# A fused linear-attention and channel-mix kernel: zero matmuls at the start, full transposes after a regrouping copy, later weight loads, and a re-tuned task order

## The chip, the cores and the metric

The kernel runs on one core of a Trainium2 chip. The metric is the device time of one execution in microseconds (us). Executions of one kernel differ, so each run is sorted into a state, "fast" or "slow" (over 1.5% above the fastest run of the same kernel). Comparisons use fast runs. Profiles give a "span", some 2 us shorter than the device time.

Engine names in the profile: PE is the matrix engine TensorE, PEld its weight loads (they overlap PE: 96.9 and 74.7 us busy in a span of 119.0 in the kernel before), DVE is VectorE, ACT is ScalarE, POOL is GpSimd, SP is the engine that only issues transfers here. "L187" is line 187 of the kernel that the profile belongs to; the same statement has other line numbers in other variants.

## The reference, cut to what matters

```python
def phi(x):                                   # q, k: (4 batches, 4 heads, 1088 tokens, 32)
    a = einsum('rd,bhsd->bhsr', S1, x)        # r = 8
    b = einsum('rd,bhsd->bhsr', S2, x)
    return outer(a, b).reshape(..., 64)
q_p, k_p = phi(q), phi(k)
kv  = einsum('bhsf,bhsd->bhfd', k_p, v);  z = k_p.sum(over tokens)
x   = (q_p @ kv) / (q_p . z + 1e-6)           # heads side by side: (4, 1088, 128)
x_prev = x shifted by one token
xk  = mu_k * x + (1 - mu_k) * x_prev;  xr likewise with mu_r
out = sigmoid(xr @ w_r) * (relu(xk @ w_k)**2 @ w_v)          # 128 -> 1024 -> 128
```

The whole k side of a batch must be summed before any x of that batch exists, and a token needs the x of its neighbour. The kernel works on two halves (two batches each), 17 tiles of 128 tokens per half, in groups of four tiles.

## The kernel before

Three parts matter. First, the loads and the transposes. k of the first half and q of the second come "head-wise" and are transposed on VectorE; k of the second half (`k1`) and q of the first (`q0`) come "token-wise" and are transposed on TensorE, one head (32 columns) at a time:

```python
    nc.gpsimd.tensor_copy(warm[:], hd["k00"][:R, 0, 0, :1])   # wait for the first tile
    load_tok("q0", q, nc.gpsimd, 1)
    load_tok("v1", v, nc.gpsimd, 1)
    nc.gpsimd.dma_start(mu_k[:], moe_mu_k.rearrange("d -> d ()"))
    nc.gpsimd.dma_start(wk[:], moe_w_k)                       # f32 to bf16 on the way
    ...
    def transp_tok(x, t0, t1):
        tp = bank["tp", x, t0] = psum.tile([P, 512], F32, name="tp", tag="aux")
        for t in range(t1 - t0):
            for h in range(H):
                nc.tensor.matmul(tp[D * h:D * h + D, t * P:t * P + P], tok[x][:, h, t0 + t, :], ident[:],
                                 skip_group_check=True, tile_position=(0, D * h))
```

Second, the names of the groups: `abp` is the projection of k, `kp` its outer product (VectorE), `kv` the accumulation, `zE` the sum z; `abwp`, `qp`, `qtp`, `xps`, `XK` are the steps from q to the mixed x; `h` is the first matmul of the channel mix, `o` the second, `rps` the gate, `osb` the output product.

Third, the order of all this is not written by hand. Each piece of work is a task with a length, needs and a priority `key`, and a small list scheduler at build time puts the tasks in a fixed order on each engine. The engines then run in that order:

```python
    PERIOD = 6.5
    for g in range(NQ):                       # a group of four query tiles
        due = (g - 1) * PERIOD - (50 if g < 2 else 0)
        task(("q1", g), "PE", 0.66 * f, ..., due - 9, opens=("aux", ("q", g)))
        task(("den", g), "DVE", 1.13, ..., due - 8)
        ...
        task(("xk", g), "DVE", 0.7, ..., due - 1, holds=[("x", g)])
    for g in range(NQ):
        x = [("xk", i) for i in range(min(g + 2, NQ))]        # the next group's x too
        for cp in range(4):
            key = g * PERIOD + cp * PERIOD / 4
            task(("mm1", g, cp), "PE", 0.43 * f, ..., x + ["dma_w"], key, opens=("h", ("h", g, cp)))
```

## Time and profile before

| | before |
|---|---|
| median of the device time | 122.8 us (121.62 to 123.44, 3 runs) |
| span of the profiled run (fast) | 119.0 us |
| TensorE busy, share of the span | 96.9 us, 81% |
| VectorE, ScalarE busy | 77.7 us, 67.3 us |
| loads done, by the 40 slices | about 28 us |

From the page of the kernel before: busy time per engine, then the span in 40 slices of 2.98 us (a digit is the busy share in tenths; PEclk the granted clock of TensorE; DMA the load of the transfer engines).

```profile
PE 96.9 (81%) x1594; PEld 74.7 (63%) x1594; DVE 77.7 (65%) x157; ACT 67.3 (57%) x117; POOL 8.9 (7%) x31
...
PE   0439998453999999799979999959969799789970
...
ACT  0402111000335477355599999777959869698950
...
PEclk9999999998699999999999999999999999999997
DMA  2999999991000000000000101002002002020212
```

TensorE is mostly full from the eleventh slice on, but not before, while the loads run. PEclk shows 9 also before the clock's first record (at 18.4 us in this trace), although the projections of that time take 423 ns a record against 278 ns for the same shape later. Before the first record the row says nothing, and the mean granted clock of a run counts that time as full speed (1.00 for 0 to 15 us in the table by windows). The next lines are from the chain of waits of the same profile (start, length, what):

```profile
20.43 0.49 PE kv L210 x21
20.93 1.59 issue
22.52 0.91 PE kv L210 x43
23.43 0.35 PE tp L169 x8
23.79 1.09 PE kv L210 x64
24.88 0.56 PE tp L169 x13
25.44 3.40 issue
28.84 1.49 PE tp L169 x19
```

Both gaps lie in the middle of a group of like matmuls, after 21 of 64 and after 13 of 32, so it is not data that is missing. Between them stand 43 + 8 + 64 + 13 = 128 matmul records, each with a weight-load record: 256. The groups of instructions, by shape (operation, output and inputs, count, then busy us and mean ns), give the price of the transposes:

```profile
L306 PE MATMUL qtp<-ident,qp 128*128 128x128 f32 x68 | 10.2, 277 | 0.0
...
L169 PE MATMUL tp<-ident,tok_q_69 128*32 128x128 f32 x136 | 6.3, 318 | 3.4 <-issue 3.4
L169 PE MATMUL tp<-ident,tok_k_68 128*32 128x128 f32 x136 | 4.5, 275 | 0.4 <-DMA tok_k_68<-in_k_dram 0.4
```

A full transpose (`qtp`) leaves one matmul record. The transpose by single heads needs four matmuls of two records each for the same tile: 272 records for 34 tiles. Why these leave two records each is not shown; they are the price seen here.

### The profile page before, as it was taken

The page shows a single profiled execution, that of the slowest core. Times are in us where ns is not written, and L with a number is a line of the kernel's source. Part 1 is how long each engine was busy: PE and PEld are TensorE (multiplying, and loading weights), DVE is VectorE, ACT ScalarE, POOL GpSimd, SP SyncE. Part 2 cuts the span into 40 slices and gives each one's busy share as a digit, 9 for nine tenths or more (in the row PEclk, how much of TensorE's full clock was granted, in tenths as well). Part 3 has the DMA queues.
Part 4 walks back from the last instruction along what each step waited for, and adds up shares of the span by engine and source line. Part 5 has one row for each costly group of instructions (what it writes and reads, how often), then busy time and mean ns, then how long its engine had stood idle before and what let it go on. Part 6 is the DMA issues. An engine that isn't in the chain of part 4 may idle for free.

```text
span 119.0 us, 3645 instructions
## 1 busy us (share of the span) xinstructions
PE 96.9 (81%) x1594; PEld 74.7 (63%) x1594; DVE 77.7 (65%) x157; ACT 67.3 (57%) x117; POOL 8.9 (7%) x31
## 2 busy tenths in 40 slices
PE   0439998453999999799979999959969799789970
PEld 0439997342788978478646777846646567556640
DVE  5465841000198993369778799859999686866870
ACT  0402111000335477355599999777959869698950
POOL 5196000050000000000000000000000000000000
PEclk9999999998699999999999999999999999999997
DMA  2999999991000000000000101002002002020212
GB/s 75 364 288 344 275 286 258 236 313 18 6 6 0 6 0 6 8 0 6 3 0 0 71 23 70 24 0 88 0 0 94 0 0 88 0 94 0 88 62 70
DMA packets 5262, 9.72 MB, mean 82 GB/s; under 512 B 1520, under 2 KB 1904, under 8 KB 5248
## 3 DMA queue, kind: packets, MB, share of 16 engines
q1 hardware_dynamic: 2976, 6.13, 16.3%
q0 software_dynamic: 1568, 1.71, 7.2%
q10 hardware_dynamic: 704, 1.67, 4.4%
q8 instruction: 12, 0.20, 0.7%
q14 instruction: 2, 0.02, 0.0%
HBM read 7.80 MB, written 2.23 MB: 84 GB/s over the span
## 4 chain that ended last, share of the span: by engine, by line
PE 56%; DMA 14%; DVE 13%; issue 7%; ACT 7%; ACTq 1%
DMA tok_k_68<-in_k_dram 14%; PE o L402 9%; PE tp L169 9%; PE h L381 8%; PE kv L210 7%; PE xps L344 6%; PE abwp L277 6%; PE qtp L306 5%; PE abp L181 4%; DVE osb L423 3%; DVE qp L189 2%; DVE XK L368 2%; DVE qpT L158 1%; PE rps L412 1%; PE rps L410 1%
## 5 line engine op out<-in xcount | busy, mean ns | idle before, releaser
L381 PE MATMUL h<-XK,wk 128*128 128x512 bf16 (+1 forms) x72 | 20.1, 367 | 3.9 <-DVE XK L368 3.2
L189 DVE TENSOR_TENSOR kp<-ab 128x1024 f32<-128x1024 f32 (+1 forms) x10 | 10.6, 1059 | 4.8 <-ACT ab L156 4.8
L156 ACT COPY ab<-abp 128x256 f32<-128x256 f32 (+1 forms) x10 | 3.4, 340 | 15.7 <-PE abp L181 15.7
L181 PE MATMUL abp<-SW,kT_136 128*128 128x64 f32 x34 | 7.8, 425 | 3.4 <-DVE kT_136 L163 3.4
L189 DVE TENSOR_TENSOR qp<-abw,an 128x1024 f32<-128x1024 f32 (+1 forms) x9 | 10.4, 1159 | 0.0
L306 PE MATMUL qtp<-ident,qp 128*128 128x128 f32 x68 | 10.2, 277 | 0.0
L344 PE MATMUL xps<-qpT,kvbd 128*64 128x256 f32 (+3 forms) x80 | 9.8, 359 | 0.1
L181 PEld LDWEIGHTS abp<-SW,kT_136 128*128 128x128 f32 x34 | 7.4, 331 | 3.7 <-DVE kT_136 L163 3.6
L381 PEld LDWEIGHTS <-wk 128*128 128x128 bf16 x72 | 5.9, 97 | 5.6 <-issue 4.7
L169 PE MATMUL tp<-ident,tok_q_69 128*32 128x128 f32 x136 | 6.3, 318 | 3.4 <-issue 3.4
L306 PEld LDWEIGHTS qtp<-ident,qp 128*128 128x128 f32 x68 | 7.8, 142 | 1.9 <-issue 0.4
L220 DVE TENSOR_TENSOR zE_140<-kv,mE 128x64 f32<-128x64 f32 x1 | 0.2, 225 | 12.9 <-PE kv L210 12.9
L210 PE MATMUL kv<-tok_v_66,kp 64*64 64x64 f32 x272 | 6.9, 261 | 1.6 <-issue 1.6
L156 ACT COPY qT_138<-tp 128x512 f32<-128x512 f32 (+1 forms) x4 | 2.0, 506 | 10.2 <-PE tp L169 10.2
L210 PEld LDWEIGHTS kv<-tok_v_66,kp 64*64 64x64 f32 x272 | 6.0, 170 | 2.7 <-issue 2.5
L423 DVE TENSOR_TENSOR osb<-o,r 128x512 f32<-128x512 f32 (+1 forms) x9 | 5.9, 658 | 1.9 <-PE o L402 1.8
L344 PEld LDWEIGHTS xps<-qpT,kvbd 128*64 128x64 f32 x80 | 4.7, 136 | 3.7 <-issue 1.0
L169 PEld LDWEIGHTS tp<-ident,tok_q_69 128*32 128x32 f32 x136 | 4.3, 127 | 4.3 <-issue 3.7
L156 ACT COPY qpT<-qtp 128x512 f32<-128x512 f32 x11 | 6.4, 597 | 0.7 <-PE qtp L306 0.7
L158 DVE COPY qpT<-qtp 128x512 f32<-128x512 f32 (+1 forms) x7 | 4.3, 614 | 2.6 <-PE qtp L306 2.6
L156 ACT COPY abw<-abwp 128x384 f32<-128x384 f32 (+1 forms) x9 | 4.2, 471 | 2.2 <-PE abwp L277 2.1
L181 PE MATMUL abp<-SW,kT_137 128*128 128x64 f32 x34 | 4.7, 278 | 0.8 <-DVE kT_137 L158 0.8
(240 smaller groups left out, 215.1 us busy)
## 6 DMA issues: line engine op xcount, KB each, us to landing
out_dram<-osb SPq DMA_DIRECT2D x7, 256.0 KB, 2.0
hd_k_70<-in_k_dram SPq DMA_DIRECT2D x1, 544.0 KB, 3.7
hd_k_71<-in_k_dram ACTq DMA_DIRECT2D x1, 544.0 KB, 5.6
tok_v_66<-in_v_dram SPq DMA_DIRECT2D x1, 544.0 KB, 8.5
tok_v_66<-in_v_dram ACTq DMA_DIRECT2D x1, 544.0 KB, 9.6
tok_k_68<-in_k_dram SPq DMA_DIRECT2D x1, 544.0 KB, 14.5
tok_k_68<-in_k_dram ACTq DMA_DIRECT2D x1, 544.0 KB, 16.8
tok_q_69<-in_q_dram SPq DMA_DIRECT2D x1, 544.0 KB
```

Source lines behind the costliest of these rows:

```text
L156: nc.scalar.copy(o, i)
L158: nc.vector.tensor_copy(o, i)
L169: nc.tensor.matmul(tp[D * h:D * h + D, t * P:t * P + P], tok[x][:, h, t0 + t, :], ident[:], skip_group_check=True, tile_position=(0, D * h))
L181: nc.tensor.matmul(p[:, t * 64:t * 64 + 64], kT[half][:, t0 + t, :], SW[:, 0, :, :2, :], skip_group_check=True)
L189: nc.vector.tensor_mul(o, _ap(a_, list(a_.ap[1:]) + [[0, R]]), _ap(b_, list(b_.ap[1:3]) + [[0, R]] + [b_.ap[3]]))
L210: nc.tensor.matmul(kv[hp:hp + 64, b2, (h // 2) * 64:(h // 2) * 64 + 64], f[rows, t - t0, h].rearrange("p i j -> p (i j)"), _ap(rhs, [[(H - ...
L277: nc.tensor.matmul(p[64 * b2:64 * b2 + 64, t * 96:t * 96 + 96], qT[half][:, T, 64 * b2:64 * b2 + 64], SW[:, 2 * half + b2].rearrange("p h ...
L306: nc.tensor.transpose(p[:, t * P:t * P + P], qp[g][:, t, 2 * pair:2 * pair + 2].rearrange("p h i j -> p (h i j)"), ident[:])
L344: nc.tensor.matmul(o[64 * pair:64 * pair + 64], kvbd[:, 2 * half + b2, pair, :], qpT[g, pair][:].rearrange("p t (b s) -> p t b s", b=2)[:, ...
L381: nc.tensor.matmul(h[:, c, :n * P], wk[:, (2 * cp + c) * P:(2 * cp + c + 1) * P], XK[:, 4 * g:4 * g + n, :].rearrange("p t s -> p (t s)"))
L402: nc.tensor.matmul(bank["o", g][:, t * P:t * P + P], k2[:, c, t * P:t * P + P], wv[:, 2 * cp + c, :], start=(cp == 0 and c == 0 and t == 0 ...
L423: nc.vector.tensor_mul(o[:, :n].rearrange("p t f -> p (t f)"), bank.pop(("o", g))[:, :n * P], rs[g][:, :n * P])
```

## The change

Its intent, in three named parts and one unnamed one: (1) 19 zero matmuls keep TensorE busy while the first tiles load; they are meant to have its clock up when work comes; (2) a ScalarE copy regroups the token-wise tiles so that a tile is transposed in one piece; (3) the weights are loaded after `v1`, in short runs, and the head tiles are padded so that their runs are short too; (4) the 20 constants of the task order are replaced by tuned ones, and the scheduler now models the buffer rings in SBUF, some of which are one buffer smaller, and starts from slightly different assumed durations and arrival times.

```diff
+    zps = psum.tile([P, 2, 512], F32, name="zps", tag="h")
+    def spin(count):
+        for _ in range(count):
+            nc.tensor.matmul(zps[:, 0, :], zero[:, :P], zero[:], skip_group_check=True)
+    spin(7)
 ...
-    wk = const.tile([P, DFF], BF16)
+    wk = const.tile([P, 4, 2 * P + 32], BF16)
 ...
     load_tok("v1", v, nc.gpsimd, 1)
+    nc.gpsimd.tensor_copy(warm[:], tok["v1"][:R, 0, 0, :1])       # waits for v1
     nc.gpsimd.dma_start(mu_k[:], moe_mu_k.rearrange("d -> d ()"))
-    nc.gpsimd.dma_start(wk[:], moe_w_k)
+    nc.gpsimd.dma_start(wk[:, :, :2 * P], moe_w_k.rearrange("p (c f) -> p c f", c=4))
 ...
+    spin(12)                                                     # after the matmuls on S1, S2
 ...
+        nc.scalar.copy(tall[x, t0][:, :n].rearrange("p t h d -> p h t d"), tok[x][:, :H, t0:t1, :])
 ...
-            for h in range(H):
-                nc.tensor.matmul(tp[D * h:D * h + D, t * P:t * P + P], tok[x][:, h, t0 + t, :], ident[:],
-                                 skip_group_check=True, tile_position=(0, D * h))
+            nc.tensor.transpose(tp[:, t * P:t * P + P], tall[x, t0][:, t].rearrange("p h d -> p (h d)"), ident[:])
 ...
+    K = dict(k1=-14.04, k1s=2.47, t=-25.79, q0=-80.88, q0s=14.85, early=55.2, q1=-10.84, den=-22.35, qp=-21.71, qt=-6.7,
+             num=-4.63, xp=7.46, xk=-15.83, gate=5.96, fin=-38.43, mm1=-1.19, mm2=-20.64, sq=-8.85, tq=86.38, P=3.65)
 ...   (every key is now written with these; rings of SBUF buffers are modelled like those of PSUM)
-    slots = {"aux": [0.0] * 2, "o": [0.0] * 2, "h": [0.0] * 2}
+    rings = dict(aux=2, o=2, h=2, tall=3, ab=3, kp=3, abw=3, an=3, qp=2, qpT0=2, qpT1=2, k1=3, k2=3, r=3)
```

More of the change, by code (lines that the diff above doesn't have):

```diff
@@ L67 @@
     tok = {x: const.tile([P, H + (x[0] == "v"), NT, D], F32, name="tok_" + x) for x in ("v0", "v1", "k1", "q0")}
-    hd = {x: const.tile([P, 2, NT, D], F32, name="hd_" + x) for x in ("k00", "k01", "q10", "q11")}
+    hd = {x: const.tile([P, 2, NT + 1, D], F32, name="hd_" + x) for x in ("k00", "k01", "q10", "q11")}
     def load_tok(x, src, eng, b2):
@@ L74, in load_hd @@
     def load_hd(x, src, eng):
-        eng.dma_start(hd[x][:], src[2 * int(x[1]) + int(x[2])].rearrange("h (a c t) d -> (h a) c t d", a=32, c=2))
+        eng.dma_start(hd[x][:, :, :NT], src[2 * int(x[1]) + int(x[2])].rearrange("h (a c t) d -> (h a) c t d", a=32, c=2))
+    zero = const.tile([P, 512], BF16)
+    nc.gpsimd.memset(zero[:], 0.0)
+    zps = psum.tile([P, 2, 512], F32, name="zps", tag="h")
[3 more added lines that the diff above has]
+    spin(7)
     S8 = const.tile([R, 2, D], F32)
@@ L163, in transp_hd, with regroup @@
             nc.vector.transpose(dst[:, t0:t1, 64 * b2 + c:64 * b2 + 64:2], hd[x][:, c, t0:t1, :])
+    tall = {}
+    def regroup(x, t0, t1):
+        n = t1 - t0
+        tall[x, t0] = work.tile([P, 4, H, D], F32, name="tall", tag="tall", bufs=3)
+        nc.scalar.copy(tall[x, t0][:, :n].rearrange("p t h d -> p h t d"), tok[x][:, :H, t0:t1, :])
     def transp_tok(x, t0, t1):
@@ L193, in k_feat @@
         ab = kab.pop((half, gi))
-        kp[half, gi] = work.tile([P, 4, H, R, R], F32, name="kp", tag="kp", bufs=4)
+        kp[half, gi] = work.tile([P, 4, H, R, R], F32, name="kp", tag="kp", bufs=3)
         outer(kp[half, gi][:, :n], ab[:, :n, :, 0, :], ab[:, :n, :, 1, :])
@@ L380, in mm1 @@
         for c in range(2):
-            nc.tensor.matmul(h[:, c, :n * P], wk[:, (2 * cp + c) * P:(2 * cp + c + 1) * P],
+            nc.tensor.matmul(h[:, c, :n * P], wk[:, cp, c * P:c * P + P],
                              XK[:, 4 * g:4 * g + n, :].rearrange("p t s -> p (t s)"))
@@ L385, in relu @@
         n = qn[g]
-        k1s[g, cp] = work.tile([P, 2, 512], BF16, name="k1", tag="k1", bufs=4)
+        k1s[g, cp] = work.tile([P, 2, 512], BF16, name="k1", tag="k1", bufs=3)
         nc.scalar.activation(k1s[g, cp][:, :, :n * P], bank.pop(("h", g, cp))[:, :, :n * P], RELU)
@@ L391, in square @@
         k1 = k1s.pop((g, cp))
-        k2s[g, cp] = work.tile([P, 2, 512], BF16, name="k2", tag="k2", bufs=4)
+        k2s[g, cp] = work.tile([P, 2, 512], BF16, name="k2", tag="k2", bufs=3)
         nc.vector.tensor_mul(k2s[g, cp][:, :, :n * P], k1[:, :, :n * P], k1[:, :, :n * P])
@@ L421, in fin @@
         n = qn[g]
-        o = work.tile([P, 4, P], F32, name="osb", tag="osb", bufs=3)
+        o = work.tile([P, 4, P], F32, name="osb", tag="osb", bufs=2)
         nc.vector.tensor_mul(o[:, :n].rearrange("p t f -> p (t f)"), bank.pop(("o", g))[:, :n * P], rs[g][:, :n * P])
@@ L435, with task @@
     tasks = {}
-    def task(name, eng, length, fn, need=(), key=0.0, opens=None, holds=()):
+    def task(name, eng, length, fn, need=(), key=0.0, opens=(), holds=()):
         tasks[name] = dict(eng=eng if isinstance(eng, tuple) else (eng,), len=length, fn=fn, need=list(need),
-                           key=key, opens=opens, holds=list(holds))
-    EV = {"ACT": 0.49, "DVE": 0.60}
-    arrive = {"S": 4.6, "k00": 5.5, "k01": 5.5, "v0": 8.5, "k1": 11.5, "q0": 14.5, "v1": 17.5, "q10": 19.0, "q11": 21.0,
-              "w": 24.0}
+                           key=key, opens=list(opens), holds=list(holds))
+    K = dict(k1=-14.04, k1s=2.47, t=-25.79, q0=-80.88, q0s=14.85, early=55.2, q1=-10.84, den=-22.35, qp=-21.71, qt=-6.7,
+             num=-4.63, xp=7.46, xk=-15.83, gate=5.96, fin=-38.43, mm1=-1.19, mm2=-20.64, sq=-8.85, tq=86.38, P=3.65)
+    EV = {"ACT": 0.50, "DVE": 0.62}
+    arrive = {"S": 4.6, "k00": 5.5, "k01": 5.5, "v0": 8.5, "k1": 11.5, "q0": 14.5, "v1": 17.5, "q10": 20.0, "q11": 22.0,
+              "w": 27.0}
     for x, t in arrive.items():
@@ L452 @@
             f = (t1 - t0) / 4
-            base = -100 + 4 * gi if half == 0 else -14 + 4 * gi
+            base = -100 + 4 * gi if half == 0 else K["k1"] + K["k1s"] * gi
             if half == 0:
@@ L456 @@
             else:
-                task(("ttk", gi), "PE", 0.86 * f, lambda e, t0=t0, t1=t1: transp_tok("k1", t0, t1), ["dma_k1"], base - 3,
-                     opens=("aux", ("tp", "k1", t0)))
+                task(("rk", gi), "ACT", 0.55 * f, lambda e, t0=t0, t1=t1: regroup("k1", t0, t1), ["dma_k1"], base + K["t"] - 1,
+                     opens=[("tall", ("tall", "k1", t0))])
+                task(("ttk", gi), "PE", 0.44 * f, lambda e, t0=t0, t1=t1: transp_tok("k1", t0, t1), [("rk", gi)], base + K["t"],
+                     opens=[("aux", ("tp", "k1", t0))])
@@ L459 @@
                 task(("ttke", gi), ("ACT", "DVE"), EV, lambda e, t0=t0, t1=t1: transp_out(e, kT[1], "k1", t0, t1),
-                     [("ttk", gi)], base - 3, holds=[("tp", "k1", t0)])
+                     [("ttk", gi)], base + K["t"], holds=[("tp", "k1", t0)])
+                tasks["ttk", gi]["holds"] += [("tall", "k1", t0)]
                 src = [("ttke", gi)]
             task(("kpj", half, gi), "PE", 0.89 * f, lambda e, h=half, g=gi: k_proj(h, g), src + ["dma_S"], base,
-                 opens=("o", ("ab", half, gi)))
+                 opens=[("o", ("ab", half, gi))])
@@ L464 @@
             task(("kab", half, gi), ("ACT", "DVE"), {"ACT": .27, "DVE": .33}, lambda e, h=half, g=gi: k_ab(e, h, g),
-                 [("kpj", half, gi)], base, holds=[("ab", half, gi)])
-            task(("kp", half, gi), "DVE", 1.15 * f + .05, lambda e, h=half, g=gi: k_feat(h, g), [("kab", half, gi)], base)
+                 [("kpj", half, gi)], base, holds=[("ab", half, gi)],
+                 opens=[("ab", ("abs", half, gi))])
+            task(("kp", half, gi), "DVE", 1.15 * f + .05, lambda e, h=half, g=gi: k_feat(h, g), [("kab", half, gi)], base,
+                 holds=[("abs", half, gi)], opens=[("kp", ("kps", half, gi))])
@@ L467 @@
             task(("kacc", half, gi), "PE", 1.15 * f, lambda e, h=half, g=gi: k_acc(h, g),
                  [("kp", half, gi), f"dma_v{half}"] + ([("kacc", half, gi - 1)] if gi else []), base,
-                 opens=("h", ("kv", half)) if gi == 0 else None, holds=[("kv", half)])
-        base = -80 if half == 0 else 4
+                 opens=[("h", ("kv", half))] if gi == 0 else (), holds=[("kv", half), ("kps", half, gi)])
+        base = -80 if half == 0 else K["k1"] + 4.5 * K["k1s"]
         task(("kz", half), "DVE", 0.22, lambda e, h=half: k_z(h), [("kacc", half, len(GR) - 1)], base, holds=[("kv", half)])
-        task(("kw", half), "PE", 0.3, lambda e, h=half: k_w(h), [("kz", half)], base, opens=("aux", ("w", half)))
+        task(("kw", half), "PE", 0.3, lambda e, h=half: k_w(h), [("kz", half)], base, opens=[("aux", ("w", half))])
@@ L477 @@
         f = (t1 - t0) / 4
-        task(("ttq", t0), "PE", 0.86 * f, lambda e, t0=t0, t1=t1: transp_tok("q0", t0, t1), ["dma_q0"], -78 + 6 * i,
-             opens=("aux", ("tp", "q0", t0)))
+        task(("rq", t0), "ACT", 0.55 * f, lambda e, t0=t0, t1=t1: regroup("q0", t0, t1), ["dma_q0"], K["q0"] - 1 + K["q0s"] * i,
+             opens=[("tall", ("tall", "q0", t0))])
+        task(("ttq", t0), "PE", 0.44 * f, lambda e, t0=t0, t1=t1: transp_tok("q0", t0, t1), [("rq", t0)], K["q0"] + K["q0s"] * i,
+             opens=[("aux", ("tp", "q0", t0))], holds=[("tall", "q0", t0)])
         task(("ttqe", t0), ("ACT", "DVE"), EV, lambda e, t0=t0, t1=t1: transp_out(e, qT[0], "q0", t0, t1), [("ttq", t0)],
-             -78 + 6 * i, holds=[("tp", "q0", t0)])
+             K["q0"] + K["q0s"] * i, holds=[("tp", "q0", t0)])
     for pc, (t0, t1) in enumerate(((9, NT), (0, 9))):
@@ L484 @@
             task(("tq", pc, b2), "DVE", 0.72, lambda e, b2=b2, t0=t0, t1=t1: transp_hd(qT[1], f"q1{b2}", t0, t1),
-                 [f"dma_q1{b2}"], -2 + 2 * pc + b2)
-    PERIOD = 6.5
+                 [f"dma_q1{b2}"], K["tq"] + 2 * pc + b2)
+    PERIOD = K["P"]
     for g in range(NQ):
         f = qn[g] / 4
-        due = (g - 1) * PERIOD - (50 if g < 2 else 0)
+        due = (g - 1) * PERIOD - (K["early"] if g < 2 else 0)
         need = []
@@ L496 @@
         halves = sorted({q_tile(4 * g + t)[0] for t in range(qn[g])})
-        task(("q1", g), "PE", 0.66 * f, lambda e, g=g: q_proj(g), dict.fromkeys(need), due - 9, opens=("aux", ("q", g)))
-        task(("q1e", g), ("ACT", "DVE"), {"ACT": .38, "DVE": .48}, lambda e, g=g: q_ab(e, g), [("q1", g)], due - 9,
-             holds=[("q", g)])
-        task(("den", g), "DVE", 1.13, lambda e, g=g: q_den(g), [("q1e", g)], due - 8)
-        task(("qp", g), "DVE", 1.15 * f + .05, lambda e, g=g: q_feat(g), [("den", g)], due - 7)
+        task(("q1", g), "PE", 0.83 * f, lambda e, g=g: q_proj(g), dict.fromkeys(need), due + K["q1"], opens=[("aux", ("q", g))])
@@ new lines @@
+        task(("q1e", g), ("ACT", "DVE"), {"ACT": .38, "DVE": .48}, lambda e, g=g: q_ab(e, g), [("q1", g)], due + K["q1"],
+             holds=[("q", g)], opens=[("abw", ("abw", g))])
+        task(("den", g), "DVE", 1.13, lambda e, g=g: q_den(g), [("q1e", g)], due + K["den"], holds=[("abw", g)],
+             opens=[("an", ("an", g))])
+        task(("qp", g), "DVE", 1.15 * f + .05, lambda e, g=g: q_feat(g), [("den", g)], due + K["qp"],
+             holds=[("abw", g), ("an", g)], opens=[("qp", ("qp", g))])
@@ L502 @@
         for pair in range(2):
-            task(("qt", g, pair), "PE", 0.44 * f, lambda e, g=g, r=pair: q_tr(g, r), [("qp", g)], due - 5,
-                 opens=("aux", ("t", g, pair)))
+            task(("qt", g, pair), "PE", 0.44 * f, lambda e, g=g, r=pair: q_tr(g, r), [("qp", g)], due + K["qt"],
+                 opens=[("aux", ("t", g, pair))], holds=[("qp", g)])
             task(("qte", g, pair), ("ACT", "DVE"), EV, lambda e, g=g, r=pair: q_trout(e, g, r), [("qt", g, pair)],
-                 due - 5, holds=[("t", g, pair)])
+                 due + K["qt"], holds=[("t", g, pair)], opens=[(f"qpT{pair}", ("qpT", g, pair))])
@@ L507 @@
         task(("num", g), "PE", 0.88 * f, lambda e, g=g: q_num(g), [("qte", g, 0), ("qte", g, 1)] + [("kkv", h) for h in halves],
-             due - 3, opens=("aux", ("x", g)))
-        task(("xp", g), "ACT", 1.1, lambda e, g=g: x_prev(g), [("num", g), "dma_w"], due - 2, holds=[("x", g)])
-        task(("xk", g), "DVE", 0.7, lambda e, g=g: x_mix(g), [("xp", g)] + ([("xp", g - 1)] if g else []), due - 1,
+             due + K["num"], opens=[("aux", ("x", g))], holds=[("qpT", g, 0), ("qpT", g, 1)])
@@ L511 @@
+        task(("xp", g), "ACT", 1.1, lambda e, g=g: x_prev(g), [("num", g), "dma_w"], due + K["xp"], holds=[("x", g)])
+        task(("xk", g), "DVE", 0.7, lambda e, g=g: x_mix(g), [("xp", g)] + ([("xp", g - 1)] if g else []), due + K["xk"],
              holds=[("x", g)])
@@ L516 @@
             key = g * PERIOD + cp * PERIOD / 4
-            task(("mm1", g, cp), "PE", 0.43 * f, lambda e, g=g, c=cp: mm1(g, c), x + ["dma_w"], key, opens=("h", ("h", g, cp)))
-            task(("relu", g, cp), "ACT", 0.92 * f, lambda e, g=g, c=cp: relu(g, c), [("mm1", g, cp)], key, holds=[("h", g, cp)])
-            task(("sq", g, cp), "DVE", 0.6 * f, lambda e, g=g, c=cp: square(g, c), [("relu", g, cp)], key)
-            task(("mm2", g, cp), "PE", 0.45 * f, lambda e, g=g, c=cp: mm2(g, c),
-                 [("sq", g, cp)] + ([("mm2", g, cp - 1)] if cp else []), key,
-                 opens=("o", ("o", g)) if cp == 0 else None, holds=[("o", g)])
@@ L523 @@
-        task(("gate", g), "PE", 0.45 * f, lambda e, g=g: gate(g), x + ["dma_w"], g * PERIOD + 3, opens=("aux", ("r", g)))
-        task(("sig", g), "ACT", 0.5 * f, lambda e, g=g: sigm(g), [("gate", g)], g * PERIOD + 3, holds=[("r", g)])
-        task(("fin", g), "DVE", 0.6 * f, lambda e, g=g: fin(g), [("mm2", g, 3), ("sig", g)], g * PERIOD + 7, holds=[("o", g)])
+            task(("mm1", g, cp), "PE", 0.43 * f, lambda e, g=g, c=cp: mm1(g, c), x + ["dma_w"], key + K["mm1"], opens=[("h", ("h", g, cp))])
@@ new lines @@
+            task(("relu", g, cp), "ACT", 0.92 * f, lambda e, g=g, c=cp: relu(g, c), [("mm1", g, cp)], key + K["mm1"], holds=[("h", g, cp)],
+                 opens=[("k1", ("k1", g, cp))])
+            task(("sq", g, cp), "DVE", 0.6 * f, lambda e, g=g, c=cp: square(g, c), [("relu", g, cp)], key + K["sq"],
+                 holds=[("k1", g, cp)], opens=[("k2", ("k2", g, cp))])
+            task(("mm2", g, cp), "PE", 0.45 * f, lambda e, g=g, c=cp: mm2(g, c),
+                 [("sq", g, cp)] + ([("mm2", g, cp - 1)] if cp else []), key + K["mm2"],
+                 opens=[("o", ("o", g))] if cp == 0 else (), holds=[("o", g), ("k2", g, cp)])
@@ L527 @@
+        task(("gate", g), "PE", 0.45 * f, lambda e, g=g: gate(g), x + ["dma_w"], g * PERIOD + K["gate"], opens=[("aux", ("r", g))])
+        task(("sig", g), "ACT", 0.5 * f, lambda e, g=g: sigm(g), [("gate", g)], g * PERIOD + K["gate"], holds=[("r", g)],
+             opens=[("r", ("rs", g))])
+        task(("fin", g), "DVE", 0.6 * f, lambda e, g=g: fin(g), [("mm2", g, 3), ("sig", g)], g * PERIOD + K["fin"], holds=[("o", g), ("rs", g)])
     HOP = 0.2
-    slots = {"aux": [0.0] * 2, "o": [0.0] * 2, "h": [0.0] * 2}
@@ L529 @@
-    turn = {r: 0 for r in slots}
+    rings = dict(aux=2, o=2, h=2, tall=3, ab=3, kp=3, abw=3, an=3, qp=2, qpT0=2, qpT1=2, k1=3, k2=3, r=3)
+    held = {r: [None] * n for r, n in rings.items()}
+    turn = dict.fromkeys(rings, 0)
     users = {}
     for n, t in tasks.items():
-        if t["opens"]:
-            users.setdefault(t["opens"][1], set()).add(n)
-        for b_ in t["holds"]:
-            users.setdefault(b_, set()).add(n)
+        for b_ in [b_ for _, b_ in t["opens"]] + t["holds"]:
+            users.setdefault(b_, []).append(n)
@@ L536 @@
     done, free, order = {}, {e: 0.0 for e in ("PE", "ACT", "DVE", "DMA")}, []
-    held = {r: [None] * len(s) for r, s in slots.items()}
     where = {}
@@ L551, in ready @@
             at = max(at, done[d] + (HOP if where[d] != e else 0.05))
-        if t["opens"]:
-            r = t["opens"][0]
+        for r, _ in t["opens"]:
             old = held[r][turn[r] % len(held[r])]
@@ L574 @@
         ln = t["len"][e] if isinstance(t["len"], dict) else t["len"]
-        if t["opens"]:
-            r, b_ = t["opens"]
+        for r, b_ in t["opens"]:
             held[r][turn[r] % len(held[r])] = b_
```

## The prediction

> **What bounds it now.**
> (1) Loading, 0 to 29 us. In the table by windows the DMA engines are full from 5 to 28 us, TensorE is busy only 1.5, 2.2, 5.0, 4.6, 3.4 and 1.6 us of each 5 us. Its k projections start at 7.85 us at half speed: a 128x64 f32 record takes 421 ns, against 278 ns for the other half's later. The chain of waits then has two gaps put down to "issue", 1.59 us at 20.9 and 3.40 us at 25.4. Both fall inside a group of like matmuls, so no semaphore explains them, and 256 TensorE records lie between them. I read them as instruction fetches queued behind the loads: queue 8 carries 12 instruction packets of 16 KB. [...]
> (2) 30 to 80 us: TensorE busy 9.1 to 10 of every 10 us; the chain is TensorE throughout.
> (3) 80 to 119 us: mixed; VectorE 9.6 of 10 at 80 to 90, TensorE idle about 8 us, and in the last 9 us busy only 5.
>
> **What the change does.**
> - Full transposes: four tiles take 1.01 us as 16 matmuls of 32 columns (tp), and would take 0.44 us as four transposes (qtp). 8.5 groups save 4.8 us of TensorE, about 3 of them after the loads.
> - Regrouping costs ScalarE 8.5 copies of 128x512, about 0.58 us each by its other copies: 5 us, mostly while it idles (busy at most 1.5 of each 5 us before 30 us).
> - 19 zero matmuls of 128x512. [...] The zeros may delay the first projection by 0.5 to 1.5 us, but then projections cost 0.85 us a group instead of 1.71 and kv accumulations 1.09 instead of 1.6 to 2.0. VectorE's feature products (1.23 us each) then set the pace. I expect the first kv group at 12.5 instead of 14.9 us.
> - Weights after v1: 0.7 MB of cast loads leave the busy stretch, so k1, q0 and v1 land 1 to 2 us sooner.
> - Task order is re-tuned. kvbd's clearing now stands behind the late weight issues on GpSimd and may hold ScalarE until about 25 us.
>
> **On the critical path.** The fetch stalls stay: TensorE just reaches the same record counts (about 449 and 705) earlier[...]. But the second boundary now lies behind the whole first kv half and 13 transposed tiles. So at 26 us the kernel stands where it stood at 32: 6 us gained. Another 3 from later transposes, and 1 to 3 from the order in stage 3.
>
> **Predicted: 112.0 us, 8 in 10 within 107.0 to 117.0.** Faster by over 2%: 0.94; within 2%: 0.04; slower: 0.02.
>
> **Signs.** First projections at 278 ns; tp groups 0.45 us; still one or two issue gaps of 2 to 4 us before 27 us; the first z product (31.0 us before) at 20 to 26; TensorE busy about 92 us, ScalarE 72.
>
> **What would break it.** Zeros that delay projections by over 2 us; a stall that halves the clock again; ScalarE waiting for kvbd or regroup buffers; a tuned order that misfits the real durations, so stage 3 idles more than 10 us.

That the zeros bring faster records, and that the stalls stay, were my estimates. The sum: the median of 122.8 us shown above, less 6, 3 and 1 to 3 us, comes to 110.8 to 112.8, and was put at 112.0. "A stall that halves the clock again" refers to the trace of the kernel before: its clock's record is at half from 28.6 to 32.0 us, behind the gap of 3.40 us.

## The result, and the profile after

| | before | changed |
|---|---|---|
| median | 122.21 us (4 runs) | 107.25 us (106.56 to 109.86, 4 runs) |
| ratio of fast runs | | 0.8832 (95%: 0.8754 to 0.891) |
| TensorE, VectorE, ScalarE busy | 96.9, 77.7, 67.3 us | 95.0, 77.8, 70.3 us |

Ratios are computed as the mean time of one kernel's fast runs over that of the other's in the same rounds, so they are not quite the ratio of the medians. The profiled run of the changed kernel was a slow one (109.86 us); so was that of a repeat (110.13 us). Where it matters below, fast profiles of close relatives are used.

The same page lines of the changed kernel (slices of 2.69 us):

```profile
PE 95.0 (88%) x1365; PEld 71.6 (66%) x1375; DVE 77.8 (72%) x160; ACT 70.3 (65%) x124; POOL 10.6 (10%) x33
...
PE   5999990598789999976999999999999999999850
...
ACT  0500410830293533767699999989999998999940
...
PEclk9999999679955699999999999999999999999999
DMA  0999999994990000000000000200202002122221
```

Over the last twenty slices TensorE is at 9 nearly throughout; before, it was not. Early on it is busy with zeros, then idle in slices 7 and 8. The timeline of TensorE in the changed kernel shows what it does there (start, length, instructions; in brackets the idle time before and what ended it):

```profile
10.17 3.68 PE L198 MATMUL abp<-SW,kT_159 128*128 128x64 f32 x32
13.78 1.16 PE L227 MATMUL kv<-tok_v_66,kp 64*64 64x64 f32 x64
...
15.24 1.16 PE L227 MATMUL kv<-tok_v_66,kp 64*64 64x64 f32 x64
19.99 1.11 PE L187 MATMUL tp<-ident,tall 128*128 128x128 f32 x4 [3.59 <-ACT tall L182]
21.03 1.99 PE L227 MATMUL kv<-tok_v_66,kp 64*64 64x64 f32 x64
...
25.77 0.78 PE L198 MATMUL abp<-SW,kT_160 128*128 128x64 f32 x6
27.60 0.43 PE L198 MATMUL abp<-SW,kT_160 128*128 128x64 f32 x2 [1.05 <-issue]
```

The same projections in the kernel before:

```profile
7.85 7.09 PE L181 MATMUL abp<-SW,kT_136 128*128 128x64 f32 x32 [3.41 <-DVE kT_136 L163]
```

The first projections are twice as fast as before (32 records in 3.68 instead of 7.09 us) but start at 10.17 instead of 7.85 us. What was won by 16.4 us is then spent on a wait of 3.59 us for `k1`, regrouped. After it TensorE is slow again (the `kv` group of 64 takes 1.99 us at 21.0, against 1.16 at 15.2; the clock's record is at half from 19.6 to 23.0 us). One "issue" gap is left.

The best single cut through these profiles is the first mixed x tile. From the timeline of VectorE of the kernel before:

```profile
46.56 0.62 DVE L368 SCALAR_TENSOR_TENSOR XK<-xps,mu_k,PP_156 128x384 bf16<-128x384 f32 x1 [1.60 <-ACT XB_154 L363]
...
115.80 0.42 DVE L423 TENSOR_TENSOR osb<-o,r 128x256 f32<-128x256 f32 x1 [0.49 <-PE o L402]
```

and of the changed kernel:

```profile
47.27 0.62 DVE L385 SCALAR_TENSOR_TENSOR XK<-xps,mu_k,PP_179 128x384 bf16<-128x384 f32 x1 [1.38 <-ACT XB_177 L380]
...
104.53 0.42 DVE L440 TENSOR_TENSOR osb<-o,r 128x256 f32<-128x256 f32 x1 [0.49 <-PE o L419]
```

In the profiled (slow) run the changed kernel has no lead at all at its first x tile; the whole gain lies after it, 57.26 instead of 69.24 us. In a fast run its span is 105.0 us, 2.7 us shorter; as the second stretch has the same length in every profile with this order, fast or slow (table below), I estimate its first x tile at about 44.6 us there.

### The profile page after: what moved, and what is told of

Same layout as the page of the kernel before. It is cut to its first block, busy times and chain, and to the rows that moved or that the text cites. A ratio compares the mean times of both kernels' runs of the same rounds, so it can differ in the third digit from the quotient of the medians.

```text
span 107.7 us, 3217 instructions
## 1 busy us (share of the span) xinstructions
PE 95.0 (88%) x1365; PEld 71.6 (66%) x1375; DVE 77.8 (72%) x160; ACT 70.3 (65%) x124; POOL 10.6 (10%) x33
## 4 chain that ended last, share of the span: by engine, by line
PE 50%; DMA 19%; ACT 13%; issue 5%; POOL 4%; DVE 3%; SPq 3%; ACTq 0%; POOLq 0%
DMA tok_v_67<-in_v_dram 19%; PE o L419 10%; PE h L398 8%; PE xps L361 8%; PE qtp L323 7%; PE abwp L294 7%; PE tp L187 3%; PE kv L227 3%; PE abp L198 2%; SPq L71 2%; ACT r L435 1%; ACT PP_179 L379 1%; DVE osb L440 1%; ACT k_1507 L404 1%; PE rps L427 1%
## 5 line engine op out<-in xcount | busy, mean ns | idle before, releaser
L398 PE MATMUL h<-XK,wk 128*128 128x512 bf16 (+1 forms) x62 | 17.6, 366 | 0.2
L187 PE MATMUL tp<-ident,tall 128*128 128x128 f32 x34 | 6.9, 340 | 4.1 <-ACT tall L182 4.1
L84 PE MATMUL zps<-zero 128*128 128x512 bf16 x19 | 7.6, 578 | 1.3 <-POOL zero L79 1.3
L187 PEld LDWEIGHTS tp<-ident,tall 128*128 128x128 f32 x34 | 4.7, 172 | 4.9 <-ACT tall L182 4.3
L198 PE MATMUL abp<-SW,kT_160 128*128 128x64 f32 x34 | 5.5, 304 | 1.0 <-issue 1.0
L198 PEld LDWEIGHTS abp<-SW,kT_160 128*128 128x128 f32 x34 | 5.1, 225 | 1.6 <-issue 1.6
L182 ACT COPY tall<-tok_k_68 128x512 f32<-128x512 f32 (+1 forms) x5 | 2.7, 556 | 5.1 <-DMA tok_k_68<-in_k_dram 5.1
L84 PEld LDWEIGHTS <-zero 128*128 128x128 bf16 x19 | 2.4, 135 | 5.3 <-issue 3.6
L435 ACT ACTIVATE r<-rps 128x512 f32<-128x512 f32 (+1 forms) x9 | 5.5, 610 | 0.0
L168 ACT COPY abw<-abwp 128x384 f32<-128x384 f32 x6 | 2.9, 482 | 3.4 <-PE abwp L294 3.4
## 6 DMA issues: line engine op xcount, KB each, us to landing
tok_k_68<-in_k_dram ACTq DMA_DIRECT2D x1, 544.0 KB, 16.5
```

The costliest lines, as they stand in the source:

```text
L84: nc.tensor.matmul(zps[:, 0, :], zero[:, :P], zero[:], skip_group_check=True)
L168: nc.scalar.copy(o, i)
L187: nc.tensor.transpose(tp[:, t * P:t * P + P], tall[x, t0][:, t].rearrange("p h d -> p (h d)"), ident[:])
L198: nc.tensor.matmul(p[:, t * 64:t * 64 + 64], kT[half][:, t0 + t, :], SW[:, 0, :, :2, :], skip_group_check=True)
L398: nc.tensor.matmul(h[:, c, :n * P], wk[:, cp, c * P:c * P + P], XK[:, 4 * g:4 * g + n, :].rearrange("p t s -> p (t s)"))
```

## The experiments

Twelve runs were made beside the first measurement, one of them the changed kernel again. The table collects the cut at the first x tile, read as in the two fences above; it leaves out "records first", which ran once, for its profile. Medians include slow runs, ratios do not. Ratios are to the kernel before in the same rounds.

| run | median us | ratio | first x tile | last output product | between | state of profile |
|---|---|---|---|---|---|---|
| before | 122.21 | 1 | 46.56 | 115.80 | 69.24 | fast |
| changed | 107.25 | 0.8832 | 47.27 | 104.53 | 57.26 | slow |
| changed, again | 107.51 | 0.8956 | 47.55 | 104.80 | 57.25 | slow |
| no zeros | 107.9 | 0.8945 | 45.35 | 102.61 | 57.26 | fast |
| weights early | 107.27 | 0.8865 | 49.57 | 106.83 | 57.26 | slow |
| old transposes | 114.03 | 0.9426 | 51.43 | 108.67 | 57.24 | fast |
| old order | 115.44 | 0.9543 | 44.57 | 110.15 | 65.58 | fast |
| new order only | 117.55 | 0.9508 | 53.02 | 110.27 | 57.25 | fast |
| x one group earlier | 114.71 | none | 46.10 | 109.99 | 63.89 | slow |
| zeros in the wait | 109.99 | 0.8876 | 44.98 | 102.25 | 57.27 | fast |
| kvbd early | 106.54 | 0.8879 | 43.89 | 101.14 | 57.25 | fast |
| k1 first | 106.28 | 0.8858 | 43.80 | 101.03 | 57.23 | fast |
| k1 first, no zeros | 105.15 | 0.8766 | 42.66 | 99.89 | 57.23 | fast |

Every kernel with the new order needs 57.2 to 57.3 us for the second stretch, whatever its transposes, zeros or loads. So with the new order nothing else that was varied reaches the second stretch. With the old order it does: there the new operations shorten it from 69.24 to 65.58 us. Left untested is the scheduler itself: the modelled rings, the smaller buffers and the changed durations were never undone alone.

### One part undone at a time

What a part is worth is given below as a difference of medians from different rounds. By the ratios, taken against the changed kernel's two (0.8832 and 0.8956), the old transposes cost 5.7 to 7.2 us and the old order 7.1 to 8.6 us.

No zeros: both calls of `spin` deleted.

```diff
-    spin(7)
-    spin(12)
```

> The changed kernel without its 19 zero matmuls, all else the same. Theory A (zeros are off the path): the first projections take 421 ns a record again and the first kv group starts near 14.9 instead of 13.8 us, but TensorE stood idle from 16.5 to 20.0 us for the regrouped k1 anyway, so the time stays at 106 to 108.5 us. Rival (the warm clock is a main part of the gain): 109.5 us or more.

107.9 us, ratio 0.8945. Theory A holds: that ratio lies between the two that the changed kernel itself got in its two sets of rounds (0.8832 and 0.8956), so the zeros gain about a per cent at most, and not measurably.

Old transposes: the loop over heads is back and `regroup` emits nothing; its tasks stay, so that the order is the same.

```diff
-        nc.scalar.copy(tall[x, t0][:, :n].rearrange("p t h d -> p h t d"), tok[x][:, :H, t0:t1, :])
+        pass
-            nc.tensor.transpose(tp[:, t * P:t * P + P], tall[x, t0][:, t].rearrange("p h d -> p (h d)"), ident[:])
+            for h in range(H):
+                nc.tensor.matmul(tp[D * h:D * h + D, t * P:t * P + P], tok[x][:, h, t0 + t, :], ident[:], ...)
```

> The changed kernel with the 32-column transposes of before and no regrouping; the order of tasks is kept. My sum: TensorE gets 4.8 us more work, ScalarE 5 us less; with TensorE busy 9.8 of 10 us after 60 us, 3 to 5 us of it show: 110 to 112 us. Rival (ScalarE is as full as TensorE, and the extra hop costs what the transposes save): within 1 us of the changed kernel.

114.03 us, so the transposes are worth 6.8 us (114.03 less 107.25), more than my 3 to 5. The table by windows shows the two terms, TensorE's time in `tp` (second number after the window's length) from 16 us to the first x tile. Old transposes first:

```profile
16.00:51.43 35.43, 10.33 (x272) 7.64 (x272) 2.76 (x4) 2.87 (x6) 0.90 0.43 89
```

and the run without zeros, which has the full transposes and a fast profile:

```profile
16.00:45.35 29.35, 6.01 (x34) 4.00 (x34) 2.75 (x4) 2.87 (x6) 0.94 0.50 106
```

The work differs by 4.3 us, near the 4.8 that were predicted. The rest is idle time: TensorE's waits in front of its groups in that stretch add up to 5.5 us with the old transposes (3.1 of them "issue" before `kv`, 2.4 mostly for `k1`) and 3.4 us without the zeros (2.2 and 1.2). All transposes come before the first x tile in this order, so none of it can hide. The rival (the hop through ScalarE eats the gain) falls.

Weights early: the wait for `v1`, the padding and the short runs taken back.

```diff
-    nc.gpsimd.tensor_copy(warm[:], tok["v1"][:R, 0, 0, :1])
-    nc.gpsimd.dma_start(wk[:, :, :2 * P], moe_w_k.rearrange("p (c f) -> p c f", c=4))
+    nc.gpsimd.dma_start(wk[:].rearrange("p c f -> p (c f)"), moe_w_k)
-    hd = {x: const.tile([P, 2, NT + 1, D], ...)}
+    hd = {x: const.tile([P, 2, NT, D], ...)}
```

> The changed kernel with the weight loads where they stood before, in long runs, no wait for v1, head tiles without padding. Theory A: in the two profiles k1 lands equally late (16.8 and 16.5 us after issue), so nothing is lost, and the 3.7 us that ScalarE waits for the clearing of kvbd are gone: 106 to 108 us. Rival (late weights and short runs keep the loads and the instruction fetches short): 109 us or more, with longer issue gaps before 30 us.

107.27 us, ratio 0.8865, between the changed kernel's two ratios. This part changes nothing that can be measured.

Old order: the 20 constants set to the values of the kernel before; all operations and the modelled rings stay.

```diff
-    K = dict(k1=-14.04, k1s=2.47, ... P=3.65)
+    K = dict(k1=-14, k1s=4, t=-3, q0=-78, q0s=6, early=50, q1=-9, den=-8, qp=-7, qt=-5,
+             num=-3, xp=-2, xk=-1, gate=3, fin=7, mm1=0, mm2=0, sq=0, tq=-2, P=6.5)
```

> The changed kernel with the 20 order constants set to what the kernel before used; all operations new. The prediction gave the order 1 to 3 us: 108.5 to 110.5 us. Rival (the order is the largest part, since the first x tile is mixed at 47 us in both profiles and the lead appears only after that): 113 us or more.

115.44 us: the order constants are worth 8.2 us, and the rival holds. From the table by windows, the second stretch (length, then TensorE, its weight loads, VectorE, ScalarE busy) of the kernel before:

```profile
46.56:115.80 69.24, 62.08 (x829) 44.23 (x818) 54.68 (x104) 54.19 (x87) 0.00 (x0) 1.00 0.08 30
```

of the old order with the new operations:

```profile
44.57:110.15 65.58, 56.91 (x642) 40.18 (x651) 54.16 (x106) 53.02 (x83) 0.00 (x0) 1.00 0.09 31
```

and of the changed kernel:

```profile
47.27:104.53 57.26, 54.20 (x634) 39.35 (x644) 51.03 (x103) 52.84 (x84) 0.00 (x0) 1.00 0.10 36
```

Old against new order: TensorE is busy 2.7 us less after the first x tile (56.91 against 54.20), in part because some transposes and projections came earlier and in part because the same kind of record took less busy time each (`qtp`: 8.7 us for 56 records against 7.1 us for 52); and its idle time in the stretch falls from 8.7 to 3.1 us (length less busy time). Together that is the 8.3 us of the stretch. (The two traces lack 9 and 10 of the 72 `h` records, so both idle times are too long by some amount.) The longest of TensorE's waits in the old-order run, from 40 us on (total, times, longest):

```profile
PE h L398 <- DVE XK L385: 4.2, 4, 1.4
```

This, the first matmul of a group waiting for the mixed x of the next one, is 3.2 us in the kernel before and is absent with the new order.

### The order alone, and one guess about it

New order only: the changed kernel with all three named parts undone at once, as in the diffs above.

> The kernel before with nothing of the three named parts: no zeros, 32-column transposes, weights early in long runs; only the new order and its modelled buffer rings. If the parts simply add (order 8.2 us, transposes 6.8 us, zeros and weights none, from the first four runs), it takes 113.5 to 115.5 us, and TensorE's waits for the mixed x tile (3.2 us before) are gone. If the order pays only together with the short transposes, it takes 118 us or more.

The fast runs, 115.62 and 114.82 us (mean 115.2), are about where adding the parts puts them, 0.9508 of before, or about 6 us won. (Two of the four runs were slow, which puts the median at 117.55.) The waits for the mixed x are gone. The table shows what the new order does: alone it makes the first x tile 6.5 us later (53.02 against 46.56), where 256 of the 272 `kv` records of the second half stand before that tile, against 137 before, and it then saves 12 us.

x one group earlier: the old constants, with those of the query chain lowered by one period.

```diff
-    K = dict(..., q1=-9, den=-8, qp=-7, qt=-5, num=-3, xp=-2, xk=-1, ...)
+    K = dict(..., q1=-15.5, den=-14.5, qp=-13.5, qt=-11.5, num=-9.5, xp=-8.5, xk=-7.5, ...)
```

> The old order constants in the changed kernel, but the seven of the query chain (projection to mixed x) lowered by one period of 6.5. Theory B (the old order loses because the first matmul of a group waits for the mixed x of the next group, 4.2 us in the run with the old order): these waits fall under 1.5 us and the time to 108 to 112 us from 115.4. Rival (the gain lies in the joint tuning of all constants): 113 us or more.

The wait did vanish, but this one stands in its place (TensorE's waits from 40 us on):

```profile
PE h L398 <- ACT k L404: 2.2, 3, 1.0
```

Only one run was fast (112.25 us), the others took 114.5 to 115.1; no ratio was computed. So theory B is half right: the late x is a real wait, but removing it alone wins at most 3 of the 8 us (on one fast run); ScalarE's relu, which frees the `h` banks, is then the next to wait for. Which of the other constants carry the rest was not settled.

### Are the "issue" gaps instruction fetches?

Records first: the kernel before, with 20 tiny matmuls (40 records) in front of everything, while TensorE has nothing to do.

```diff
+    for _ in range(20):
+        nc.tensor.matmul(zps[:2, 0, :1], zero[:], zero[:, :1], skip_group_check=True)
```

> The kernel before with 20 tiny matmuls (40 records, one column each) ahead of everything, while TensorE idles. Theory (instruction fetch): the two issue gaps stay at the same count of TensorE records, after the 449th and 705th, so each falls 40 records earlier in the program: the first about 43 records into the kv group of 128 that followed the first k1 transposes instead of 63, the second already at the end of the next kv group, before the 13 tile matmuls. Rival (a wait of the program, for data or a buffer): the gaps stay before the same instructions as before, at 489 and 745 records.

TensorE's timeline of this run (a single one of 122.05 us, its state unknown, made for the profile):

```profile
23.22 0.43 PE L174 MATMUL tp<-ident,tok_q 128*32 128x128 f32 x8
23.58 1.08 PE L215 MATMUL kv<-tok_v,kp 64*64 64x64 f32 x57
28.06 0.34 PE L215 MATMUL kv<-tok_v,kp 64*64 64x64 f32 x7 [3.40 <-issue]
```

The long gap now comes after 57 of the 64 `kv` records; before, it came after all 64 and 13 `tp` records more. That is 7 + 13 = 20 matmul records earlier in the program, exactly the number put in front, and the same count from the start. The gap is as long (3.40 us) and has moved to another instruction, which a wait of the program cannot do. The first gap shrank to 0.3 us, which I had not expected, but it too stands at the same count, after the first record of its `kv` group.

The same rule holds between other runs. Without the 19 zeros the gap in the `kv` group comes after 50 records, with them after 31 (both shown below). These kernels are otherwise alike up to that group.

The traces settle it further; the times of single transfer packets stand in them. Counting all records of TensorE's two rows (matmuls and weight loads, and the few semaphore records of its sequencer), all 17 issue gaps over 0.25 us on TensorE, spread over twelve profiles, lie after record 449, 705 or 1729, that is at steps of 256. In every one TensorE resumes 1.25 to 1.55 us after a 16 KB instruction packet on queue 8 has ended (in the kernel before at 21.16 and 27.50 us, with TensorE back at 22.52 and 28.84; in the changed one at 26.17, back at 27.60). So the gaps are instruction fetches.

That the loads make the fetch late is not shown. In the kernel before, the next packet starts 4.0 us after TensorE resumes at 22.5 us, with loads running, but 1.0 us after it resumes at 28.8 us, with the loads over; this fits, yet no run varied the loads alone. And a fetch can stall without them: this gap of the old transposes stands at record 1729, where the transfer engines are busy for 2% of the time (from 43 to 46 us).

```profile
45.66 0.45 PE L227 MATMUL kv<-tok_v,kp 64*64 64x64 f32 x12 [1.08 <-issue]
```

### What to do about the wait for k1

Zeros in the wait: kvbd is cleared before GpSimd waits for its loads (see the next run), and 14 more zero matmuls stand in front of the first transposes.

```diff
+        if (x, t0) == ("k1", 0):
+            spin(14)
```

> The changed kernel with kvbd cleared ahead of GpSimd's wait for v1, and 14 more zero matmuls where TensorE waits for k1 (16.2 to 20.0 us). Theory C (what separates the slow from the fast runs here is the half clock after that idle stretch): no half-clock window at 19.6 to 23.0 us, mean granted clock at least 0.98, 104.5 to 106.5 us with less spread. Rival (the half clock falls where TensorE is not the limit): 107 us as before.

The clock did stay up: PEclk on this run's page is 9 in all slices, and the mean granted clock of the profiled run 0.999.

The two fast runs took 107.57 and 107.55 us, as before; by the ratio (0.8876) they equal kvbd early (0.8879), the kernel that differs from this one in the 14 zeros alone. So the time is the rival's, but its reason, that the half clock costs nothing here, is not shown. The 14 zeros are 28 more records ahead of the second instruction block (record 705), and TensorE waits for that block here, which kvbd early does not:

```profile
27.62 0.33 PE L229 MATMUL kv<-tok_v,kp 64*64 64x64 f32 x4 [2.41 <-issue]
```

What the full clock may have won, this wait took back. The other two runs were slow (112.4 and 113.2 us, mean granted clock 0.938 and 0.939). They were not profiled, so why is open.

The changed kernel once more:

> The changed kernel once more, unaltered, for a fast profile and as the measure of the other three. 106.5 to 108 us in its fast runs; from the first mixed x tile to the last output 57.2 us, as in every profile with the new order so far, and so a first mixed x tile at 44.5 to 45.5 us.

107.51 us, 0.8956; the second stretch took 57.25 us, as expected. The profile was a slow one again, so it could not test the first x tile of a fast run.

kvbd early. In the changed kernel the chain of waits runs through GpSimd:

```profile
3.90 20.57 DMA tok_v_67<-in_v_dram
...
25.08 0.56 POOL mu_k L118
...
27.47 0.90 POOL wv L122
28.36 0.55 POOL kvbd L158
...
28.93 0.26 ACT kvbd L256
```

The clearing of `kvbd` stands behind the wait for `v1` and five weight issues, and ScalarE waits 3.7 us for it.

```diff
+    kvbd = const.tile([P, B, 2, 2 * D], F32)
+    nc.gpsimd.memset(kvbd[:], 0.0)
     nc.gpsimd.tensor_copy(warm[:], hd["k00"][:R, 0, 0, :1])
```

> The changed kernel with kvbd cleared before GpSimd waits for the loads. The chain of waits of the changed kernel runs through that clearing (ScalarE waits 3.7 us for it), but TensorE itself waits only 0.46 us behind it. Theory (the chain there has almost no slack to give): 0 to 1 us faster than the changed kernel. Rival (the chain tells the truth, the whole wait counts): 2 us or more faster.

106.54 us, all four runs fast, against 107.45 us, the mean of the three fast runs of the changed kernel in the same rounds: 0.9 us of a wait of 3.7. The chain was right about the place but had a nearly as long path beside it.

k1 first: in addition, the second halves of `q0` and `v1` are issued on ScalarE's queue, behind k1.

```diff
     load_tok("k1", k, nc.scalar, 1)
+    load_tok("q0", q, nc.scalar, 1)
+    load_tok("v1", v, nc.scalar, 1)
 ...
-    load_tok("q0", q, nc.gpsimd, 1)
-    load_tok("v1", v, nc.gpsimd, 1)
```

> As a5, with the second halves of q0 and v1 issued on ScalarE's queue behind k1 instead of on GpSimd's queue beside it. Theory (k1 lands at 19.3 us only because q0 and v1 share the engines with it): k1 lands by 16 us, TensorE's wait of 3.6 us before its first transposes falls under 1.5 us, but the fetch at record 449 then stalls it, so only 0.5 to 2 us are won: 105 to 106.5 us. Rival (the later landing of q0 or v1 costs as much): 107 us or more.

The later half of k1 landed 11.2 us after its issue instead of 15.3 (kvbd early). The first line is from the transfers of kvbd early, the second fence from k1 first (KB, us to landing):

```profile
tok_k<-in_k_dram ACTq DMA_DIRECT2D x1, 544.0 KB, 15.3
```

```profile
tok_k<-in_k_dram ACTq DMA_DIRECT2D x1, 544.0 KB, 11.2
```

In both runs the transfer engines were busy (the DMA row is at 9 from the second to the eighth slice, 2.6 to 20.8 us), so what GpSimd issued beside k1 had delayed k1, by about 4.1 us. The theory's time holds (106.28 us), but against kvbd early that is only 0.3 us less, and the runs of the two overlap (105.73 to 106.79 and 106.17 to 106.82). The fetch took the wait over:

```profile
16.78 0.66 PE L187 MATMUL tp<-ident,tall 128*128 128x128 f32 x4
17.36 0.69 PE L227 MATMUL kv<-tok_v,kp 64*64 64x64 f32 x31
21.14 1.22 PE L227 MATMUL kv<-tok_v,kp 64*64 64x64 f32 x33 [3.08 <-issue]
```

k1 first, no zeros: as above, without both calls of `spin`.

> As c2 without the zero matmuls. If the zeros were useless in the changed kernel only because k1 came late, they matter here: 1 to 2 us slower than c2. If instruction fetches limit the early stage anyway, within 0.7 us of c2.

```profile
20.48 1.02 PE L225 MATMUL kv<-tok_v,kp 64*64 64x64 f32 x50
22.90 0.45 PE L225 MATMUL kv<-tok_v,kp 64*64 64x64 f32 x14 [1.40 <-issue]
```

105.15 us: the zeros do not help here, they cost 1.1 us. Neither of the two expectations had that sign. With the zeros TensorE arrives sooner, stalls 3.08 us for instructions, and loses its clock. It resumes 1.8 us earlier than without them (21.14 against 22.90), yet starts `wps`, some 120 matmuls on, 1.1 us later (28.18 against 27.04). This is PEclk of k1 first, then of the run without zeros.

```profile
PEclk9999999955799999999999999999999999999996
```

```profile
PEclk9999999999999999999999999999999999999998
```

In the first, two to three slices after the stall run at about half clock (5, 5 and 7 tenths), and in them work was waiting. Without zeros TensorE runs slowly up to about 20 us (its `kv` groups of 64 take 1.99 us at 15.0 and 17.6 us, 1.16 at 23.9; the clock's first record is at 20.4 us, so the row's earlier 9s say nothing), arrives later, stalls 1.40 us, and keeps its clock from there on. This version is the fastest of all, correct, and all four of its runs were fast (105.01 to 105.37 us).

## Why the prediction was right or wrong

The time was inside the range, near its fast end: 107.25 us against 112.0 (107.0 to 117.0), and the call "faster" was right. That it fell inside is partly luck: the early gain was counted too high and the order far too low, and the two errors offset each other. The sum was put together wrongly, in this way:

- "1 to 3 from the order in stage 3": mis-sized. The order is worth 8.2 us with the other parts in place and about 6 us alone. I had read TensorE's idle time after 80 us but not that before it, and had not counted that a different order also lowers TensorE's busy time in the second stretch (by 2.7 us).
- Transposes, "save 4.8 us of TensorE": the term was right as work (4.3 us measured), but undoing them costs 6.8 us, since fewer records and earlier work also cut waits. "Another 3 from later transposes" is wrong in place: all of it falls before the first x tile.
- Zeros: their effect on TensorE was right (273 ns a record in the first projections instead of 423, by the groups of instructions; without the zeros the 32 records take 7.09 us again), the gain was not. The first kv group came at 13.78, not 12.5 us; the zeros held the first projection back by 2.3 us, more than the 2 us that the prediction named as breaking it; and the lead ran into the wait for k1. Worth nothing here.
- "k1, q0 and v1 land 1 to 2 us sooner": wrong. The later half of k1 landed 16.8 us after its issue at 2.48 before, and 16.5 after its issue at 2.76 now: 19.3 us in both. Nor did the others: the halves that GpSimd issues landed at 15.2 and 15.6 us (q0) and at 19.5 us in both (v1).
- "The fetch stalls stay": right. The fetch was tested (records first), its being queued behind the loads was not; and the packet of each fetch itself takes only 0.9 to 1.7 us. One gap of 1.05 us is left in the profile, smaller than the 2 to 4 us foretold, because the wait for k1 covers the first fetch.
- kvbd holding ScalarE: right in kind, until 28.9 us rather than 25. It costs 0.9 us.
- "At 26 us the kernel stands where it stood at 32: 6 us gained": not a sound measure. In z it looked true (first z product at 25.42 instead of 31.04 us, as foretold), but the first x tile, which the second stretch waits for, gained only about 2 us in fast runs by the estimate above, as the new order had put other work first.
- Other signs held: ScalarE busy 70.3 us (72 foretold); TensorE 95.0 us in the slow profile and 93.1 in the fast profile of kvbd early (92 foretold).

## What to carry to other kernels

Cut two profiles at a point that all later work waits for, and compare the parts: here one number, constant to 0.1 us over ten profiles, showed that with the new order the second stretch no longer depends on anything else that was varied. A gain ahead of a wait is worth only what the wait leaves of it, so move the data or the instructions before warming the clock (with k1 late the zeros gained nothing measurable, 107.25 against 107.9 us; with k1 first they cost 1.1). A gap put down to nothing, in mid-group and at a fixed count of records, was an instruction fetch in all 17 cases here; fewer records, or a lighter load of transfers at that moment, are means to try; neither was tested alone here.

## What the runs show of the fetches and the clock

- Instruction fetches: 256 records lie between the two gaps of the kernel before, and the 17 gaps, of 0.3 to 3.4 us, were not hidden behind work; 16 of them came while loads ran or had just ended, and one of 1.08 us long after.
- Activity and the clock: in the kernel before, 7 us of f32 projections, recorded as busy throughout, ran at 423 ns a record to their end, and the clock's first record comes at 18.4 us. So a stretch that the profile shows as busy need not bring the full clock; why is not shown. In the changed kernel the second batch of zeros ran slowly from 5.88 to about 9.3 us (weight loads 0.43 us apart until then; the clock's first record, at full, is at 9.34), and the first, of 3.1 us, had not brought the full clock.
- Idleness and the clock: 3.59 us (changed) and 3.08 us (k1 first) of idleness were each followed by a slow stretch, but so were 2.14 us (no zeros) and 1.75 and 2.09 us (new order only), while 2.41 us (zeros in the wait) was not. The length of the gap alone does not tell them apart.
- Warming TensorE with zeros cost 1.1 us in k1 first, where it then waited longer (3.08 instead of 1.40 us) and ran at half clock at a worse moment.
